# Two of sixteen gates on GpSimd, global q and k loaded to the quarters, and GpSimd's clearing ahead of its loads

## The chip, the core and the metric

The kernel runs on one core of a Trainium2 chip. A core has five engines that run their own instruction streams in order: PE (TensorE, matmuls), DVE (VectorE), ACT (ScalarE), POOL (GpSimd) and SP (SyncE, which issues DMAs). PE writes into PSUM; its weight loads are shown as PEld. GpSimd works on SBUF only and has no operand in PSUM in this kernel. Transfers are issued by SP, ACT or POOL and carried out by sixteen DMA engines. Engines wait for each other by semaphores.

The metric is the device time of one execution in microseconds, as the median of several runs.

## The reference

Eight batches, eight heads, 512 local tokens and 32 global tokens per batch, head dimension 64. Local tokens attend to the global tokens and to a window of 32 tokens on each side; global tokens attend to everything. The joined result goes through a two-layer network with a hard-swish gate.

```
s_g  = scale * q_g @ [k_g, k_l]^T          out_g = softmax(s_g) @ [v_g, v_l]
s_l  = scale * q_l @ [k_g, k_l]^T          local part masked to |i - j| <= 32
out_l = softmax(s_l) @ [v_g, v_l]
x = [out_g, out_l], heads joined           # 8 * 544 rows of 512
h = x @ w_in                               # 512 -> 2048
g = h * clip(h + 3, 0, 6) / 6
out = g @ w_out                            # 2048 -> 512, float32
```

Inputs and output are float32; the kernel works in fp16 with float32 sums in PSUM.

## The kernel before

Attention and network are interleaved. For each batch the attention of the local tokens runs in four pairs of blocks (`local`: scores on PE, `tensor_tensor_reduce` with the mask on DVE for the maximum, exponential on ACT, transposes on PE, values on PE, normalising and a transpose on DVE into `xt`), the global tokens in two halves (`globe`, `globe_values`). Then the first layer of the network (`moe_first`, `first`) makes sixteen chunks of 128 hidden columns: four matmuls into a PSUM bank `m` (three banks), ACT's Relu of (h + 3) / 6 into `t1` (three buffers), and DVE's gate, min(t1, 1) * h, from `t1` and the bank into `gts`. The bank is free when the gate is done. Batch 0 does this in three parts of its tokens, as they come out of attention. The second layer (`moe_second`, `second`) sums sixteen chunks into a bank per 128 tokens, in four quarters of four chunks, copies the bank to `ot` on ACT or DVE, and SP stores it. While PE works on the network of a batch, the attention of the next batch goes on between.

The order of each engine's instructions is fixed when the program is built: a planner (`Plan.lay`) takes operations from named streams, each with a rank and estimated costs, and writes them out one after another. Where an operation may go to several engines, the planner chooses; `SPARE` is a handicap for DVE in this choice. Estimates of a load are its issue, its service and `lat`, the time until it has landed. So ranks and estimates change the order in the program, and nothing else.

Local q and k of batch 0 come in two halves. The first (chunks 0 and 1) is loaded as float32 by SP into a stage in `win`, cast by ACT and turned by DVE into `qt` and `kt`; the second is cast by the transfer itself and is issued by POOL into `wout`. Batch 1's q and k go into `xt` and `qtmp` (turned at line 590 and 595), those of later batches into `rawq` and `rawk`. POOL issues all of these and v, w_in and w_out in one stream, and in the same stream it clears buffer 1 of the keys and values (`clear`, lines 369 to 377), makes the mask's blocks (`band`) and the identity, copies v into the shifted strips `vs` (line 542; ACT and DVE may do so too for batch 0), and from batch 1 on copies key borders (`kg`).

Global q and k of batches 0 and 1 (`once`): one load of 32 rows to partitions 0 to 31, into an `ot` buffer for batch 0 and into `graw` for batch 1, and then four casts of 32 partitions, one for each quarter of `gn`. DVE turns `gn` into `kt` (line 605) and `qg` (line 601). In the program before, ACT issues both loads of batch 0 and SP both of batch 1.

Of the kernel before, what the change touches and what calls it, by code (L numbers as in the profile page):

```python
# [37 lines left out]
class Plan:  # L38
# [7 lines left out]
    SPARE, PHASES = 0.5, 9  # L46
# [146 lines left out]
def kernel(  # L193
# [13 lines left out]
    P = 128  # L207
# [38 lines left out]
    def tiles(name, n, shape, dtype, pool=None):  # L246
        return [(pool or sb).tile(shape, dtype, tag=f"{name}{i}", name=f"{name}{i}") for i in range(n)]
# [10 lines left out]
    graw0 = tiles("graw0_", 1, [W, 2, H, D], FP32)[0]  # L258
# [17 lines left out]
    t1s = tiles("t1", 3, [P, Sl], FP32)  # L276
    ots = tiles("ot", 3, [P, dm], FP32)
# [18 lines left out]
    for name, rank in (("l0", 0), ("ld", 5), ("lq", -2), ("sh", 0), ("sq", 0), ("st", 3.5), ("g0", 0), ("ga", -9), ("first", -9), ("pad", -30), ("gc", -6), ("gd", 3), ("gp", 3.9), ("cast", -5), ("msk", lambda n: 1 if n < 9 else 1.25), ("tq", lambda n: 0 if n < 8 else 3), ("kg", 0.5), ("vs", 1.5), ("clr", 1),  # L296
                       ("s", 0.5), ("mx", lambda n: 1.2 if n < 33 else 2.7), ("ex", 1.9), ("t", -0.5), ("etc", 0), ("av", -0.7), ("nm", 0.7),
                       ("xp", -0.5), ("gx", 1),
                       ("mf", lambda n: 9 + n * 1e-3), ("ms", lambda n: 9 + (n + len(PARTS) * NDFF + 2) * 1e-3), ("t1", 0), ("gate", -0.7), ("ot", 3)):
        plan.stream(name, rank)  # L300
    for name in ("l0", "ld", "lq", "sh", "st", "g0", "ga", "sq"):
        plan.stream("dq" + name, 0 if name in ("l0", "ld", "lq") else -1)
# [56 lines left out]
    def setup():  # L359
        nc.vector.memset(mxs[0], 0.0)  # L360
        clear(nc.vector, 0)
        nc.vector.memset(masks[0], 0.0)
        nc.vector.memset(masks[1][:, 0], 0.0)
        nc.vector.memset(masks[1][:, 1:, W:P - W], 0.0)
        for e in range(2):
            nc.vector.memset(mask(NU)[quarter(e, 0), 0:W], OUTSIDE)
            nc.vector.memset(mask(NU + 1)[quarter(e, 1), P - W:], OUTSIDE)

    def clear(eng, r):
        eng.memset(vg[r], 0.0)  # L370
        eng.memset(vg[r][0:W, :, D:D1], 1.0)
        for e in range(2):
            eng.memset(pairs(kt[r])[quarter(e, 0), :, 0:W, :], 0.0)
# [42 lines left out]

    def stage_loads():
# [3 lines left out]
        there = [[load("g0", "SP", 0.47, 0.65, stage[:, i, c, :], raw(src, 0)[:, c, :], lat=(2.6, 3.1, 3.2, 5.7)[2 * c + i]) for i, src in enumerate((q_l, k_l))]  # L421
# [15 lines left out]
        lower = plan.add("l0", Op(("POOL", 1.9), band))  # L437
        for i, src in enumerate((q_l, k_l)):
            st["qk"][1, i] = [load("l0", "POOL", 0.75, 1.6, nat(0, i)[:, NC // 2:, :], raw(src, 0)[:, NC // 2:, :], lat=4.2 - 0.4 * i)]
        vg_load(0, "l0")  # L440
        for m in (2, 3, NU, 1, 0, NU + 1):
            made["mask", m] = [plan.add("msk", Op(("ACT", 0.21), lambda o=o, i=i: nc.scalar.copy(out=o, in_=i), [lower])) for o, i in places(m)]
# [23 lines left out]
    def once(b, k, src, name):  # L466

        raw_ = (graw0[:, k] if b else ots[k][0:W].rearrange("g (h d) -> g h d", d=D))
        got = load("sh" if b else "ga", "SP" if b else "ACT", 0.47, 0.45 if b else 0.3, raw_, src[b].rearrange("h g d -> g h d"), [w_in_l[1][1]] if b else ())
        g = Buf("gn" + name, 1)  # L470
        state[b]["gn", k] = g
        state[b]["gl"][k] = []
        for e in range(2):
            for f in range(2):
                def cast(engine, e=e, f=f):
                    o, i = gn0[k][quarter(e, f)], raw_.rearrange("g (c e) d -> g e c d", e=2)[:, e]
                    if engine == "ACT":
                        nc.scalar.copy(out=o, in_=i)
                    else:
                        (nc.gpsimd if engine == "POOL" else nc.vector).tensor_copy(out=o, in_=i)  # L480
                op = Op({"POOL": 0.43, "ACT": 0.42} if b else {"ACT": 0.42, "DVE": 0.4} if k else {"ACT": 0.42}, None, [got], [] if e or f else [g])
                op.emit = lambda op=op, cast=cast: cast(op.engine)
                state[b]["gl"][k].append(plan.add("gp" if b else "gc" if k else "gd", op))
# [33 lines left out]
    def v_loads(b, to):  # L517
# [4 lines left out]
        if b == 0:  # L522
            made["ident"] = plan.add("clr", Op(("POOL", 0.55), lambda: make_identity(nc, ident)))
        vl = [load(to, "POOL", 0.88, 1.05 if b else 1.25, lambda j=j: v0[v.slot][:, j, :, 0:D],
                   v_l[b, :, j * P:(j + 1) * P, :].rearrange("h s d -> s h d"), lat=LATE[b] if b else 3.3 - 0.4 * j) for j in range(NJ)]
# [58 lines left out]
    def turn_words(b, st, k):  # L584
# [23 lines left out]
        def halo(c0, c1, e, engine):  # L608
            copy = nc.scalar.copy if engine == "ACT" else nc.gpsimd.tensor_copy
            line = flat(kt[k.slot])  # L610
            for f, at, frm in ((1, 0, 10), (0, 12, 2)):
                copy(out=line[quarter(e, f), c0:c1, at * W:(at + 1) * W],
                     in_=line[quarter(e, 1 - f), c0:c1, frm * W:(frm + 1) * W])
        n = 2 if b == 0 else 1
        for q in range(n):
# [10 lines left out]
            else:  # L626
                st["k"].append(plan.add("tq", Op(("DVE", 1.9 / n), lambda c0=c0, c1=c1: turn_q(c0, c1), st["qk"][q, 0],
                                                 [] if b == 0 else [k])))
                a = plan.add("tq", Op(("DVE", 1.95 / n), lambda c0=c0, c1=c1: turn_k(c0, c1), st["qk"][q, 1]))
                st["k"].append(a)  # L630
            for e in range(2):
                h = Op({"POOL": 0.55, "ACT": 0.5}, None, [a])
                h.emit = lambda h=h, c0=c0, c1=c1, e=e: halo(c0, c1, e, h.engine)
                st["halo"].append(plan.add("kg", h))
# [264 lines left out]
    def first(xfn, n, cs, gfn, deps, takes, reads):  # L899
# [11 lines left out]
        def gate():  # L911
# [5 lines left out]
             for k, c in enumerate(cs)]  # L917
        r = plan.add("t1", Op(("ACT", 0.09 + all_ * 0.00083), lambda: nc.scalar.activation(  # L918
# [33 lines left out]
    def moe_first(b):  # L952
# [4 lines left out]
        for at, part in enumerate(PARTS if b == 0 else [range(NJ)]):  # L957
# [3 lines left out]
            for c in range(0, NDFF, per):  # L961
# [3 lines left out]
                def gated(c=c, g=g, cols=cols, per=per):  # L965
# [3 lines left out]
                            deps, [g] if at == 0 and c % CG == 0 else [], [xt])  # L969
# [24 lines left out]
    with tc.manual_schedule():  # L994
        clean = plan.add("first", Op(("DVE", 0.1), lambda: nc.vector.memset(zero, 0.0)))
        plan.add("pad", Op(("PE", 4.0), lambda: [nc.tensor.matmul(out=aps[0][0:W, 0, 0:2], lhsT=zero, rhs=zero[:, 0:2], start=True, stop=True) for _ in range(100)], [clean],
# [6 lines left out]
        made["clear"] = plan.add("clr", Op(("POOL", 2.4), lambda: clear(nc.gpsimd, 1), [made["ident"]]))  # L1003
# [76 lines left out]
```

## Time and profile before

| | us |
|---|---|
| median of three runs | 327.26 (326.31 to 327.92) |
| the profiled execution | 328.56 |
| its span | 326.8 |
| busy PE / DVE / ACT / POOL | 305.8 / 258.4 / 238.3 / 157.7 |
| xt, batch 1's q: issued / landed | 19.71 / 31.05 |
| gate on DVE (line 914) | 136 of 0.682 |
| Relu on ACT (line 918) | 136 of 0.597 |
| strip copy on POOL, 1056 words | 1.062 |

Times in the profile are microseconds from the span's start. A row of a timeline gives start, length, engine, line, operation, output and input, and how many instructions it joins; in brackets stand the idle time before and what ended it. A row of groups gives the count, the busy time and the mean in ns, and after the second bar the idle time before the group. A DMA row gives the queue, how many transfers, the size, and the time from issue to landing. A stretch's row gives the busy time of PE, PEld, DVE, ACT and POOL (number of instructions in brackets), the granted clock, the share of the sixteen DMA engines, and GB/s. "issue" is time in which an engine waited for nothing that the profile shows.

### The profile page before, as it was taken

Reading aid. Unit: us, or ns where it says so; the run is one execution under the profiler, and the core shown is the slowest. Engines: PE = TensorE matmul, PEld = TensorE weight load, DVE = VectorE, ACT = ScalarE, POOL = GpSimd, SP = SyncE. Lnnn points to the kernel's source line nnn. Section 1 sums busy time; section 2 is a strip of 40 time slices with the busy share of each in tenths; the row PEclk is TensorE's granted clock in tenths of the full one; section 3 lists DMA queues with packets and bytes.
Section 4 is the critical chain, followed back from the end, with each engine's and each line's share of the span. In section 5 each row is a group of like instructions: output and inputs, shape, how many; then the busy total and the mean of one; then the engine's idle time right before and its main releaser. Section 6 shows DMA issues by size and latency. Waiting matters only on the chain.

```text
span 326.8 us, 11215 instructions
## 1 busy us (share of the span) xinstructions
PE 305.8 (94%) x4484; PEld 172.8 (53%) x4484; DVE 258.4 (79%) x913; ACT 238.3 (73%) x550; POOL 157.7 (48%) x205
## 2 busy tenths in 40 slices
PE   4477898799999999999999999999999999999995
PEld 4356784454555545555555555555455545556654
DVE  7788996789989897989998999889989985742210
ACT  7999678557895788868876997699759965643221
POOL 9999999029955935665009944963900000000000
PEclk9999999999999999999999999999999999999999
DMA  8999999959952995199949993999111012011223
GB/s 201 180 215 190 188 212 170 230 152 178 200 85 66 140 184 138 46 111 160 217 118 99 226 138 48 148 157 174 33 35 34 2 34 67 0 34 32 65 53 79
DMA packets 104821, 39.54 MB, mean 121 GB/s; under 512 B 91648, under 2 KB 97536, under 8 KB 104768
## 3 DMA queue, kind: packets, MB, share of 16 engines
q0 software_dynamic: 91392, 16.91, 63.9%
q1 hardware_dynamic: 12832, 21.78, 26.8%
q8 instruction: 35, 0.57, 0.7%
q10 hardware_dynamic: 544, 0.13, 0.2%
q14 instruction: 18, 0.15, 0.2%
HBM read 35.13 MB, written 8.91 MB: 135 GB/s over the span
## 4 chain that ended last, share of the span: by engine, by line
PE 86%; POOL 5%; DMA 3%; DVE 2%; issue 2%; ACT 0%; POOLq 0%
PE m L934 37%; PE m L907 35%; PE t L758 4%; DMA xt<-in_q_l_dram 3%; PE a L776 3%; PE s L699 3%; PE t L847 1%; POOL vs L542 1%; PE s L816 1%; POOL v L308 1%; PE a L857 1%; PE s L712 1%; POOL win L308 1%; DVE qt L590 1%; DVE kt L595 1%
## 5 line engine op out<-in xcount | busy, mean ns | idle before, releaser
L934 PE MATMUL m<-wout,gts 128*128 128x512 f16 (+1 forms) x560 | 130.8, 373 | 1.8 <-issue 1.8
L907 PE MATMUL m<-xt,win 128*128 128x512 f16 (+2 forms) x640 | 121.0, 338 | 2.2 <-DVE gts L914 1.2
L914 DVE SCALAR_TENSOR_TENSOR gts<-t,m 128x512 f16<-128x512 f32 x136 | 92.1, 682 | 34.4 <-ACT t L918 33.1
L918 ACT ACTIVATE t<-m 128x512 f32<-128x512 f32 x136 | 81.2, 597 | 34.5 <-PE m L907 31.4
L907 PEld LDWEIGHTS <-win 128*128 128x128 f16 x704 | 70.4, 114 | 48.0 <-issue 3.8
L542 POOL COPY vs<-v 32x1056 f32<-32x1056 f32 (+4 forms) x91 | 81.7, 898 | 29.1 <-DMA v<-in_v_l_dram 24.8
L749 ACT ACTIVATE ex<-sm,mx 128x128 f16<-128x128 f32 x256 | 84.9, 394 | 7.2 <-DVE mx L743 6.5
L934 PEld LDWEIGHTS <-gts 128*128 128x128 f16 x560 | 51.6, 98 | 52.1 <-issue 3.5
L743 DVE CUSTOM_DVE_ANT_0 sm<-s,mask 128x128 f32<-128x128 f32 x240 | 56.2, 285 | 7.2 <-PE s L712 4.1
L308 POOL DMA_DIRECT2D rawq<-in_q_l_dram x12 | 12.6, 1059 | 46.3 <-DVE rec L785 24.3
L318 ACT COPY et<-t 128x1024 f16<-128x1024 f16 x28 | 28.1, 1005 | 8.1 <-PE t L758 8.0
L308 POOL DMA_DIRECT2D v<-in_v_l_dram x32 | 28.2, 896 | 0.0
L942 ACT COPY ot<-m 128x512 f32<-128x512 f32 (+1 forms) x29 | 16.5, 570 | 15.3 <-PE m L934 15.2
L786 DVE TENSOR_TENSOR x<-a,rec 128x512 f16<-128x512 f32 x32 | 22.1, 692 | 1.1
L799 DVE STREAM_TRANSPOSE xt<-x 128x512 f16<-128x512 f16 x32 | 22.5, 704 | 0.1
L758 PEld LDWEIGHTS <-ex 128*128 128x128 f16 x256 | 17.3, 101 | 9.0 <-ACT ex L749 2.7
L743 DVE DVE_READ_ACCUMULATOR2_ANT mx<- 128x1 f32 x256 | 21.3, 83 | 0.0
L758 PE MATMUL t<-ident,ex 128*128 128x128 f16 x240 | 19.9, 225 | 1.5 <-ACT ex L749 1.5
L318 ACT COPY etg<-t 128x640 f16<-128x640 f16 x16 | 11.1, 692 | 10.5 <-PE t L847 10.5
L776 PEld LDWEIGHTS <-et 128*32 128x32 f16 x1024 | 10.0, 98 | 13.1 <-ACT ex L749 4.7
L646 DVE STREAM_TRANSPOSE qt<-rawq 128x512 f16<-128x512 f16 x24 | 15.5, 680 | 0.0
L650 DVE STREAM_TRANSPOSE kt<-rawk 128x512 f16<-128x512 f16 x24 | 15.5, 679 | 0.0
(92 smaller groups left out, 221.5 us busy)
## 6 DMA issues: line engine op xcount, KB each, us to landing
out_dram<-ot SPq DMA_DIRECT2D x62, 128.0 KB, 2.9
vs<-vg SPq DMA_DIRECT2D x32, 132.0 KB, 5.4
v<-in_v_l_dram POOLq DMA_DIRECT2D x32, 128.0 KB, 6.4
rawq<-in_q_l_dram POOLq DMA_DIRECT2D x12, 256.0 KB, 5.8
rawk<-in_k_l_dram POOLq DMA_DIRECT2D x12, 256.0 KB, 6.8
rawq<-rawq SPq DMA_DIRECT2D x12, 254.0 KB, 5.3
rawk<-rawk SPq DMA_DIRECT2D x12, 254.0 KB, 4.9
win<-in_moe_w_in_dram POOLq DMA_DIRECT2D x4, 512.0 KB, 11.3
```

Source lines behind the costliest of these rows:

```text
L308: eng.dma_start(out=o() if callable(o) else o, in_=i() if callable(i) else i)
L318: nc.scalar.copy(out=o(), in_=i())
L542: (nc.gpsimd if op.engine == "POOL" else nc.vector).tensor_copy(out=o(), in_=i())
L743: nc.vector.tensor_tensor_reduce(out=sms[sm.slot], in0=scored(c // 2)[:, z:z + P], in1=mask(m), scale=-scale, scalar=3.0e38, op0=ALU.add, ...
L749: nc.scalar.activation(out=exs[ex.slot][:, un, c, :], in_=sms[sm.slot], func=EXP, scale=-1.0, bias=mxs[mx.slot])
L758: nc.tensor.matmul(out=turned(tp)[:, z:z + P], lhsT=exs[ex.slot][:, un, c, :], rhs=ident, is_transpose=True)
L786: nc.vector.tensor_tensor(out=xs[x.slot].rearrange("p g (a d) -> p g a d", a=2), in0=o[:, :, 0:D].rearrange("p g (d a) -> p g a d", a=2), ...
L799: nc.vector.transpose(out=xts[xt.slot][:, :, n * P:(n + 1) * P].rearrange("p k (t q) -> p t k q", q=W), in_=xs[x.slot].rearrange("p (t k) ...
L907: nc.tensor.matmul(out=mps[ps.slot][:, k * n:(k + 1) * n], lhsT=column_tile(c)[:, m], rhs=x, start=(m == 0), stop=(m == KC - 1))
L914: nc.vector.scalar_tensor_tensor(out=g, in0=shape(t1s[t1.slot][:, 0:all_]), scalar=1.0, in1=shape(mps[ps.slot][:, 0:all_]), op0=ALU.min, o ...
L918: r = plan.add("t1", Op(("ACT", 0.09 + all_ * 0.00083), lambda: nc.scalar.activation(out=t1s[t1.slot][:, 0:all_], in_=mps[ps.slot][:, 0:al ...
L934: nc.tensor.matmul(out=mps[ps.slot][:, 0:n], lhsT=gfn(c), rhs=w_out_t[c // 4][:, c % 4, cols], start=(c == 0), stop=(c == NDFF - 1))
```

## The change

Several things change together.

- The gate of chunks 5 and 13 of every batch from 1 to 7 (`aside`, 14 gates in all) is made on GpSimd: ACT copies the bank to `t1` as it is, which frees the bank, and GpSimd makes clip(h / 6 + 0.5, 0, 1) * h in three instructions over 128 x 512, with `graw` as work space.
- Global q and k of batches 0 and 1 are loaded to all four quarters of the partitions, by four loads each of 32 rows of 4 heads (every quarter gets the even or the odd heads), and cast by one instruction of 128 partitions. For batch 0 ACT issues two of k's loads, SP two of k's and four of q's; for batch 1 SP issues all eight.
- The identity and the clearing of the second `vg` stand on GpSimd ahead of the second half loads of batch 0's q and k; the rest of the clearing of buffer 1 stands behind them and ahead of the loads of v_g, v and w_in. Before, the clearing stood behind the first w_in load.
- DVE may make mask copies (it takes 7 of 14) and key borders of batch 0. Of the strip copies of batch 0, DVE makes 8 (3 before), ACT 3 (5) and GpSimd 18 (21).
- Turns of batch 1's q stand as four instructions in place of one; three stand ahead of two gates and one behind them.
- Ranks and estimates of the planner change, and with them details of the order on PE, DVE and ACT. The number of matmuls of each kind stays.

```diff
@@ Plan
-    SPARE, PHASES = 0.5, 9
+    SPARE, PHASES = 0.8, 9
@@
-    graw0 = tiles("graw0_", 1, [W, 2, H, D], FP32)[0]
+    graw0 = tiles("graw0_", 1, [P, 2, NC, D], FP32)[0]
+    clip = graw0.rearrange("p k c d -> p (k c d)")
...
-   ("st", 3.5), ("tq", lambda n: 0 if n < 8 else 3), ("vs", 1.5), ("ex", 1.9), ("t", -0.5), ("nm", 0.7), ("xp", -0.5), ("gate", -0.7), ("ot", 3)
+   ("st", 2), ("gq", 0.1), ("tq", lambda n: 1.5 if n < 8 else 4.5), ("vs", 2.2), ("ex", 0.5), ("t", 1), ("nm", 0), ("xp", 1), ("pgate", 0.6), ("gate", -1.4), ("ot", 0)
@@ setup
-        clear(nc.vector, 0)
+        clear_globals(nc.vector, 0)
+        clear_rest(nc.vector, 0)
@@
-    def clear(eng, r):
+    def clear_globals(eng, r):
         eng.memset(vg[r], 0.0)
         eng.memset(vg[r][0:W, :, D:D1], 1.0)
+
+    def clear_rest(eng, r):
@@
+    def mask_part(o, i, lower):
+        op = Op({"ACT": 0.18, "DVE": 0.11}, None, [lower])
+        op.emit = lambda: nc.scalar.copy(out=o, in_=i) if op.engine == "ACT" else nc.vector.tensor_copy(out=o, in_=i)
+        return plan.add("msk", op)
@@ stage_loads
         lower = plan.add("l0", Op(("POOL", 1.9), band))
+        made["ident"] = plan.add("l0", Op(("POOL", 0.55), lambda: make_identity(nc, ident)))
+        plan.add("l0", Op(("POOL", 0.62), lambda: clear_globals(nc.gpsimd, 1)))
         for i, src in enumerate((q_l, k_l)):
-            st["qk"][1, i] = [load("l0", "POOL", 0.75, 1.6, ..., lat=4.2 - 0.4 * i)]
+            st["qk"][1, i] = [load("l0", "POOL", 0.75, 1.6, ..., lat=2.1 - 0.4 * i)]
+        made["clear"] = plan.add("l0", Op(("POOL", 1.9), lambda: clear_rest(nc.gpsimd, 1)))
         vg_load(0, "l0")
@@ once
-        raw_ = (graw0[:, k] if b else ots[k][0:W].rearrange("g (h d) -> g h d", d=D))
-        got = load("sh" if b else "ga", "SP" if b else "ACT", 0.47, ..., raw_, src[b].rearrange("h g d -> g h d"), ...)
-        (four casts, one for each quarter)
+        raw_ = graw0[:, k] if b else ots[k][:, 0:NC * D].rearrange("p (c d) -> p c d", d=D)
+        rows = src[b].rearrange("(c e) g d -> e g c d", e=2)
+        got = []
+        for f in range(2):
+            to, engine = ("sh", "SP") if b else ("ga", "ACT") if k and not f else ("gq", "SP")
+            got += [load(to, engine, 0.47, 0.15, raw_[quarter(e, f)], rows[e], ...) for e in range(2)]
+        def cast(engine):
+            o, i = gn0[k], raw_
...
@@ v_loads
-            made["ident"] = plan.add("clr", Op(("POOL", 0.55), lambda: make_identity(nc, ident)))
@@ turn_words (batch 1)
+                pieces = [(c0, c1)] if b == 0 else [(c, c + 1) for c in range(c0, c1)]
...
@@
+    def gate_aside(x, g):
+        nc.gpsimd.tensor_scalar(out=clip, in0=x, scalar1=1.0 / 6.0, scalar2=0.5, op0=ALU.mult, op1=ALU.add)
+        nc.gpsimd.tensor_scalar(out=clip, in0=clip, scalar1=0.0, scalar2=1.0, op0=ALU.max, op1=ALU.min)
+        nc.gpsimd.tensor_tensor(out=g, in0=clip, in1=x, op=ALU.mult)
@@ first
+        if aside:
+            r = plan.add("t1", Op(("ACT", 0.09 + all_ * 0.00083), lambda: nc.scalar.copy(out=t1s[t1.slot], in_=mps[ps.slot]), a, [t1], [ps]))
+            return plan.add("pgate", Op(("POOL", PG), lambda: gate_aside(t1s[t1.slot], gfn()), [r], takes, [t1]))
@@ moe_first
-                            deps, [g] if at == 0 and c % CG == 0 else [], [xt])
+                            deps, [g] if at == 0 and c % CG == 0 else [], [xt], b > 0 and c % 8 == 5)
@@ the program
-        made["clear"] = plan.add("clr", Op(("POOL", 2.4), lambda: clear(nc.gpsimd, 1), [made["ident"]]))
```

More of the change, by code (lines that the diff above doesn't have):

```diff
@@ L608, in halo @@
         def halo(c0, c1, e, engine):
-            copy = nc.scalar.copy if engine == "ACT" else nc.gpsimd.tensor_copy
+            copy = {"ACT": nc.scalar.copy, "POOL": nc.gpsimd.tensor_copy, "DVE": nc.vector.tensor_copy}[engine]
             line = flat(kt[k.slot])
@@ L995 @@
         clean = plan.add("first", Op(("DVE", 0.1), lambda: nc.vector.memset(zero, 0.0)))
[L996 removed]
+        plan.add("pad", Op(("PE", 1.45), lambda: [nc.tensor.matmul(out=aps[0][0:W, 0, 0:2], lhsT=zero, rhs=zero[:, 0:2], start=True, stop=True) for _ in range(100)], [clean],
                            n=200, mode=("small", "small")))
```

60 lines of the change are left out of this document (28 added, 32 removed).

## The prediction

> **What bounds the kernel now.** I read the stretches first, then the chain that ended last, then the queues of GpSimd and the DMA in the first 35 us. Busy time by stretch (columns: PE, weight loads, DVE, ACT, POOL, clock, DMA share, GB/s):
>
> ```profile
> 35.00:40.00 5.00, 3.54 (x90) 3.41 (x90) 4.97 (x12) 2.37 (x6) 4.37 (x8) 1.00 1.09 192
> ...
> 60.00:100.00 40.00, 40.00 (x601) 20.73 (x600) 35.69 (x121) 29.64 (x66) 23.59 (x26) 1.00 1.13 161
> ...
> 250.00:270.00 20.00, 20.00 (x296) 10.48 (x298) 17.54 (x64) 16.35 (x41) 0.00 (x0) 1.00 0.06 15
> ```
>
> From 60 us on PE is busy without a gap (40.00 of 40, 20.00 of 20). PE's work is the same in both kernels: each kind of matmul comes in the same number. So beyond 60 us nothing can be won, only lost. What can move is the time at which PE becomes full, near 38 us. The chain that ended last says what sets it (start, length, what):
>
> ```profile
> 19.71 11.34 DMA xt<-in_q_l_dram
> 31.08 2.08 DVE qt L590
> 33.15 1.20 DVE gts L914 x2
> 34.51 0.69 DVE x L786
> 35.20 1.98 DVE kt L595 x4
> 37.18 0.53 DVE gts L914
> 37.75 4.69 PE m L907 x56
> ```
>
> The load of batch 1's q into xt lands at 31.05. DVE had finished its work before that at 30.97, turns q (2.08 us), passes the gates that free PE's banks, and at 37.75 PE starts the run that never breaks again but for two waits ("issue", 0.92 us at 51.97 and 1.85 us at 57.24). DVE has no gap between 31 and 43.8, so whatever delays its turn of q delays PE.
>
> The load was issued 11.34 us before it landed: it stood in a queue. GpSimd's order and the DMAs' time from issue to landing:
>
> ```profile
> 2.52 0.84 POOL L308 DMA_DIRECT2D wout<-in_q_l_dram  x1
> ...
> 4.66 3.55 POOL L308 DMA_DIRECT2D v<-in_v_l_dram  x4
> 8.17 0.70 POOL L308 DMA_DIRECT2D win<-in_moe_w_in_dram  x1
> ...
> 10.07 0.30 POOL L373 MEMSET kt<- 32x256 f16 x1
> ...
> 14.80 4.96 POOL L542 COPY vs<-v 32x264 f32<-32x264 f32 x11
> ```
>
> ```profile
> win<-in_moe_w_in_dram POOLq DMA_DIRECT2D x1, 512.0 KB, 9.2
> v<-in_v_l_dram POOLq DMA_DIRECT2D x1, 128.0 KB, 7.0
> ```
>
> The last v load (issued near 7.3) lands at 14.3, the first w_in load (8.17) at 17.4, the fourth at 28.5, xt at 31.05. The DMA engines' share is above 1.0 in every stretch of 1 or 2 us from 3 to 32, so this is one full pipe, and a hole in it is not made good.
>
> **The change part by part.**
>
> Order on GpSimd. Identity and the clearing of vg (8.91 to 10.07, 1.16 us) now stand ahead of the second half loads of batch 0's q and k; the rest of the clearing (10.07 to 12.61, 2.54 us) stands ahead of v_g, v and the first w_in load. So q's half is issued at 2.52 + 1.16 = 3.7 (was 2.52), v_g at 7.8 (4.07), v from 8.4 (4.66), the first w_in at 11.9 (8.17). The second to fourth w_in loads keep 12.6 to 14.8, for the queue up to there holds the same work.
>
> What this does to the pipe: before, v landed 6.5 to 7.0 us after issue, part of it behind other loads. A v load at 53.87, with little ahead of it, took 5.5. So v now lands from 8.4 + 5.5 = 13.9 (was 11.1), and the fourth at 11.0 + 5.5 = 16.5 at best (was 14.3): 2.2 us later. The pipe has run dry meanwhile, since the half loads are through near 9 and v starts arriving past 10. The w_in loads and xt follow in the same queue at its full pace, so they keep their distances: the first w_in 3.1 us behind v (19.6), xt 13.65 us behind that (33.25). The bounds are 31.05 (no hole: the stage loads, alone now, finish early and pull all forward) and 34.3, for if v needs 6.5 us as before, the fourth lands at 17.5. I take the distances from 16.5, since an emptier queue is nearer to the 5.5 row.
>
> Global q and k to the quarters. Each of the four loads of 64 KB becomes four of 32 KB, so the rows come twice: 128 KB more for batch 0, which fit in the hole, and 128 KB more for batch 1, ahead of xt, on a pipe that moved 197 GB/s in the first 62 us: 0.65 us if all of it queued ahead of xt, nothing if it shares engines that are idle. Its packets are small and interleave with w_in's; I take 0.15, near nothing, because the strips and v's packets make the same mix before. SP issues 6 more for batch 0 and 6 more for batch 1 (0.4 to 0.8 us each), in gaps of 7.9 and 19 us between its issues there, so nothing. But batch 0's second k_g copies now queue behind the stage loads on SP: the last stage load lands at 7.6, k_g came at 4.2. The first scores (6.78) move to about 7.6; the second half of k (10.05) and ACT's queue still end that stage, so 0 on the path.
>
> Casts: 16 casts of 0.40 us become 4. ACT had 10 of them and keeps the wide 4, so it saves 6 x 0.40 = 2.4 us before 33 us; POOL saves 4 x 0.41 and DVE 2 x 0.34. DVE takes 7 of the 14 mask copies (about 0.1 each, like its mask memsets of 0.09) and 5 more strip copies (8 instead of 3, about 0.4 each, 2.0 us). None of it is ahead of xt on the path: DVE reaches the turn of q near 31 to 32.5 with or without it. DVE's strip copies now stand in order ahead of the mask-and-maximum instructions and wait for v (13.9 and 14.8, where they ran at 13.4); behind them wait the exponentials, then PE's transposes. That is up to 2.5 us lost in a chain whose ACT part has become 2.4 us shorter: hidden by xt's own lateness, and if that is absent, up to +1.
>
> Turn of q in four pieces: the fourth stands behind two gates, the gate that frees PE at 37.75 still has the same work ahead of it (6.6 us from xt's landing), 0.
>
> Two gates of sixteen, batches 1 to 7 (14 in all). DVE loses 14 x 0.682 = 9.5 us, worth nothing since PE is full. ACT's Relu of 0.597 becomes a copy of about 0.57, nothing. POOL gains 14 gates of three instructions over 128x512. No row of POOL has two inputs. The nearest rows:
>
> ```profile
> L542 POOL COPY vs<-v 32x1056 f32<-32x1056 f32 x42 | 44.6, 1062 | 26.5 <-DMA v<-in_v_l_dram 24.8
> ...
> L542 POOL COPY vs<-v 32x528 f32<-32x528 f32 x7 | 4.4, 623 | 0.3
> ```
>
> Each is between 0.62 and 1.06 us, a gate between 1.9 and 3.2; I take 0.62 + 0.62 + 1.06 = 2.3, as the third reads two tensors and so as many elements as the long copy. The Trainium skill (GPSIMD Engine Reference, 3.1 Elementwise, side by side) measures a two-input add over 2048 elements at 4497 ns, which no row here shows; by it the third would be an estimated 1.1 us and the gate 2.4, with no change in the sum. POOL has 16 of 40 us free (23.59 busy from 60 to 100). Behind a gate on POOL stand strip copies and the raw loads of later batches; the gate itself waits for ACT's copy. PE needs the last such gate (chunk 13) for the fourth quarter of a second-layer tile: two more chunks (1.7 us), three quarters (2.6 us) and two attention pieces (0.8 us), about 5.1 us after its matmuls. ACT 0.6 plus a queued copy 1.06 plus the gate 2.3 is 4.0: fits, 0. If a pair of raw loads (2 x 1.05) or several strips stand ahead, it is late by 0.5 to 1 us in a batch.
>
> DVE sharing memory ports with a busier POOL: the gate on DVE took 682 ns at 62 to 250 us with POOL half busy and 685 ns at 250 to 290 with POOL nearly idle, so 0.
>
> ```profile
> L914 DVE SCALAR_TENSOR_TENSOR gts<-t,m 128x512 f16<-128x512 f32 x86 | 58.3, 682 | 9.2 <-ACT t L918 8.1
> ```
>
> **Sum.** xt lands at 31.05 + 2.2 + 0.15 = 33.4, DVE and PE follow: +2.35 us; the rest 0. The profiled execution took 328.56 (span 326.8), which gives 330.9; it was 1.3 above the median of the runs, 327.26, so on the median I forecast 329.6. A measurement of this kernel tells about 0.5% (1.6 us) from no change.
>
> **The rivals.**
> The hole closes (no change): with q's half issued later the stage loads have the engines alone and every later transfer starts as soon as it is issued; xt is late by the 0.65 of extra rows at most, giving about 327.6. For it: half loads and v shared the engines from 5 to 14. Against: the pipe was full before, so lateness of v adds.
>
> Faster: the two issue waits at 51.97 and 57.24 (2.77 us together) are PE waiting with no engine named, at a time when v's loads at 53.87 fill the DMA queue (share above 2). If everything ahead is shifted against these loads, both waits could go. With 0.65 of extra rows that is 327.26 + 0.65 - 2.77 = 325.1. It decides only when xt is less than about 1.1 us late. Against: the order of those loads and matmuls is almost the same.
>
> Gates late on POOL: 0.5 us in each of seven batches on top of my forecast, 329.6 + 3.5 = 333.1. For it: raw loads cost 1.05 each on POOL and stand ahead of some gates; PE has no slack. Against: 16 of 40 us are free.
>
> **How the numbers follow.** Forecast 0.47, hole closes 0.24, faster 0.14, gates late 0.15. The forecast's own range goes from xt 1.1 us late to 3.9 (34.3 and all 0.65), 328.4 to 331.2; 0.41 of its 0.47 lies over +0.5%, and with the late gates slower is 0.56. The hole closing and the other 0.06 lie within 0.5%: 0.30. Faster is 0.14. The range 325.8 to 333.2 leaves out most of the faster case and the far end of late gates.
>
> **What would show it.** Step by step: v landing from 13.9, the first w_in near 19.6, xt near 33.4; DVE idle about 2 us before its turn of batch 1's q, named for that load; PE's unbroken run starting near 40; PE's total unchanged and full from 62 us; POOL gates near 2.3 us. Wrong would be: xt at 31, PE waiting after 60 us for GpSimd's gates, or the two issue waits gone.

## The result, and the profile after

The changed kernel takes 343.02 us (342.33 to 343.17), the kernel before 327.58 (326.31 to 327.92). The ratio is 1.0475, 95% interval 1.0442 to 1.0508: slower, by 15.4 us where 2.35 were forecast, and outside the range. The profiled execution took 343.17 with a span of 341.4 us, so it stands for the four runs, which lie within 0.9 us.

PE's own work is the same 1264 matmuls of the two layers in both kernels. The moments at which some of them start say in which stage the time goes. Times are from each trace's start; the 192nd matmul of the first layer is the last one of batch 0, and each later column up to the 384th adds 64, a batch. The last column is the time from the 192nd to the last matmul of the second layer.

| kernel | first layer, 1st | 192nd | 256th | 320th | 384th | second layer, last | 192nd to last |
|---|---|---|---|---|---|---|---|
| before | 24.1 | 48.1 | 86.2 | 121.7 | 157.0 | 322.6 | 274.5 |
| after | 27.6 | 51.0 | 91.9 | 131.2 | 170.1 | 336.9 | 285.9 |

So in this execution the start (up to the 192nd) is 2.9 us late, and 11.4 us are lost behind it, where I had forecast nothing. Between the 192nd and the last, PE stands idle for 8.9 us (before: 2.8).

Busy time by stretch, the same three stretches as before (columns: PE, weight loads, DVE, ACT, POOL, clock, DMA share, GB/s):

```profile
35.00:40.00 5.00, 4.06 (x93) 3.39 (x92) 4.97 (x11) 3.68 (x8) 3.17 (x5) 1.00 1.94 184
60.00:100.00 40.00, 37.12 (x469) 18.45 (x469) 28.51 (x103) 26.86 (x60) 24.98 (x26) 0.96 1.24 158
250.00:270.00 20.00, 19.89 (x276) 10.46 (x275) 17.57 (x65) 15.53 (x36) 7.90 (x8) 1.00 0.12 29
```

PE is no longer full from 60 to 100 us: 37.12 of 40, and of these a part runs at a lower clock (0.96 on the mean). The counts, 469 here and 601 before, can't be compared, since another mix of long and short matmuls falls into the 40 us.

The chain that ended last, for the start:

```profile
11.20 6.87 DMA v<-in_v_l_dram
...
20.46 0.47 DVE vs L553
...
33.87 1.57 DVE qt L601 x3
35.45 1.11 DVE gts L936 x2
...
43.44 1.91 PE m L929 x16
45.35 0.67 PE s L726 x62
```

The load of xt isn't in it, but it is no earlier: its landing isn't recorded in this trace, but GpSimd's next load, which waits for it, starts at 34.08, so xt landed near 33.8 (an estimate: 0.28 us lie between the two without the gates, where the landing is recorded). The chain that is shown came at the same moment. v lands at 18.07, DVE's strip copies wait for it, and the attention of batch 0 behind them reaches the turn of batch 1's q at 33.87. PE comes to the scores of batch 1 at 45.35; before, this stood at 42.44, again 2.9 us later.

The groups of the new gate on GpSimd, and the gate on DVE (count, busy us, mean ns, then the idle time before):

```profile
L936 DVE SCALAR_TENSOR_TENSOR gts<-t,m 128x512 f16<-128x512 f32 x122 | 82.6, 683 | 51.2 <-ACT t L943 50.1
L917 POOL TENSOR_SCALAR graw<-t 128x512 f32<-128x512 f32 x14 | 8.6, 613 | 36.5 <-ACT t L941 35.7
L918 POOL TENSOR_SCALAR graw<-graw 128x512 f32<-128x512 f32 x14 | 26.8, 1916 | 1.2
L919 POOL TENSOR_TENSOR gts<-graw,t 128x512 f16<-128x512 f32 x14 | 17.8, 1271 | 1.2
```

A gate is 0.61 + 1.92 + 1.27 = 3.80 us, not 2.3: the instruction with the maximum and minimum takes three times the one with the multiplication and addition. What one such gate does, from the timeline of batch 1 (start, length, engine, line; in brackets the idle time before and what ended it):

```profile
79.38 0.59 ACT L941 COPY t<-m 128x512 f32<-128x512 f32 x1 [0.27 <-PE m L929]
...
79.98 1.06 POOL L553 COPY vs<-v 32x1056 f32<-32x1056 f32 x1
...
81.13 0.61 POOL L917 TENSOR_SCALAR graw<-t 128x512 f32<-128x512 f32 x1
81.83 1.93 POOL L918 TENSOR_SCALAR graw<-graw 128x512 f32<-128x512 f32 x1
83.84 1.26 POOL L919 TENSOR_TENSOR gts<-graw,t 128x512 f16<-128x512 f32 x1
...
85.13 0.60 ACT L943 ACTIVATE t<-m 128x512 f32<-128x512 f32 x1 [2.39 <-POOL gts L919]
...
85.76 0.69 DVE L936 SCALAR_TENSOR_TENSOR gts<-t,m 128x512 f16<-128x512 f32 x1 [2.31 <-ACT t L943]
...
86.50 1.02 PE L929 MATMUL m<-xt,win 128*128 128x512 f16 x4 [1.81 <-DVE gts L936]
...
87.86 4.44 PE L929 MATMUL m<-xt,win 128*128 128x512 f16 x12
```

ACT's copy is ready at 79.97, GpSimd makes a strip first, and the gate ends at 85.10. It holds one of the three t1 buffers as long, so the fourth Relu of ACT behind that copy waits 2.39 us, DVE's gate behind it 2.31, and PE 1.81 for a free bank. After that the twelve matmuls from 87.86 take 4.44 us, 0.37 each, where four just before took 1.02 (0.26). The granted clock had fallen, to 0.50 from 87.86 to 91.27:

```profile
84.00:88.00 4.00, 2.19 (x41) 1.01 (x39) 1.81 (x3) 2.63 (x5) 3.94 (x6) 0.98 1.17 172
88.00:92.00 4.00, 4.00 (x12) 1.45 (x12) 2.54 (x18) 1.80 (x5) 3.72 (x5) 0.59 1.83 197
```

The same happened once more, from 128.82 to 132.23; an estimate from half the clock over these 6.8 us is 3.4 us of PE's time. Over the whole execution ACT waited for GpSimd's gates six times, 9.3 us in all, 2.6 the longest.

### The profile page after: what moved, and what is told of

The parts are those of the page before. It is cut to its first block, busy times and chain, and to the rows that moved or that the text cites. A ratio compares the mean times of both kernels' runs of the same rounds, so it can differ in the third digit from the quotient of the medians.

```text
span 341.4 us, 11276 instructions
## 1 busy us (share of the span) xinstructions
PE 312.1 (91%) x4484; PEld 174.3 (51%) x4484; DVE 249.1 (73%) x906; ACT 234.8 (69%) x539; POOL 210.1 (62%) x242
## 4 chain that ended last, share of the span: by engine, by line
PE 60%; POOL 19%; issue 7%; DVE 6%; DMA 4%; ACT 3%; POOLq 0%; ACTq 0%; DVEq 0%
PE m L959 28%; PE m L929 22%; POOL vs L553 5%; POOL graw L918 5%; POOL gts L919 3%; PE t L772 3%; PE a L790 2%; DMA v<-in_v_l_dram 2%; POOL v L309 2%; DMA wout<-in_k_l_dram 2%; DVE gts L936 2%; POOL graw L917 1%; DVE sm L757 1%; ACT t L943 1%; PE t L861 1%
## 5 line engine op out<-in xcount | busy, mean ns | idle before, releaser
L929 PE MATMUL m<-xt,win 128*128 128x512 f16 (+2 forms) x640 | 126.5, 346 | 5.4 <-DVE gts L936 4.9
L936 DVE SCALAR_TENSOR_TENSOR gts<-t,m 128x512 f16<-128x512 f32 x122 | 82.6, 683 | 51.2 <-ACT t L943 50.1
L943 ACT ACTIVATE t<-m 128x512 f32<-128x512 f32 x122 | 72.5, 599 | 46.7 <-PE m L929 34.5
L929 PEld LDWEIGHTS <-win 128*128 128x128 f16 x704 | 71.3, 115 | 53.6 <-issue 11.0
L553 POOL COPY vs<-v 32x1056 f32<-32x1056 f32 (+5 forms) x88 | 80.4, 913 | 8.9 <-DMA v<-in_v_l_dram 4.2
L319 ACT COPY et<-t 128x1024 f16<-128x1024 f16 x31 | 31.3, 1011 | 7.4 <-PE t L772 7.4
L967 ACT COPY ot<-m 128x512 f32<-128x512 f32 (+1 forms) x34 | 19.5, 574 | 16.7 <-PE m L959 16.2
L917 POOL TENSOR_SCALAR graw<-t 128x512 f32<-128x512 f32 x14 | 8.6, 613 | 36.5 <-ACT t L941 35.7
L918 POOL TENSOR_SCALAR graw<-graw 128x512 f32<-128x512 f32 x14 | 26.8, 1916 | 1.2
L919 POOL TENSOR_TENSOR gts<-graw,t 128x512 f16<-128x512 f32 x14 | 17.8, 1271 | 1.2
```

Source lines behind the costliest of these rows:

```text
L319: nc.scalar.copy(out=o(), in_=i())
L553: (nc.gpsimd if op.engine == "POOL" else nc.vector).tensor_copy(out=o(), in_=i())
L918: nc.gpsimd.tensor_scalar(out=clip, in0=clip, scalar1=0.0, scalar2=1.0, op0=ALU.max, op1=ALU.min)
L919: nc.gpsimd.tensor_tensor(out=g, in0=clip, in1=x, op=ALU.mult)
L929: nc.tensor.matmul(out=mps[ps.slot][:, k * n:(k + 1) * n], lhsT=column_tile(c)[:, m], rhs=x, start=(m == 0), stop=(m == KC - 1))
L936: nc.vector.scalar_tensor_tensor(out=g, in0=shape(t1s[t1.slot][:, 0:all_]), scalar=1.0, in1=shape(mps[ps.slot][:, 0:all_]), op0=ALU.min, o ...
```

## The experiments

Each ratio is to runs of the kernel before on the same chip.

### What is slow in the gate: the two one-input instructions exchanged

```diff
-        nc.gpsimd.tensor_scalar(out=clip, in0=x, scalar1=1.0 / 6.0, scalar2=0.5, op0=ALU.mult, op1=ALU.add)
-        nc.gpsimd.tensor_scalar(out=clip, in0=clip, scalar1=0.0, scalar2=1.0, op0=ALU.max, op1=ALU.min)
+        nc.gpsimd.tensor_scalar(out=clip, in0=x, scalar1=-3.0, scalar2=3.0, op0=ALU.max, op1=ALU.min)
+        nc.gpsimd.tensor_scalar(out=clip, in0=clip, scalar1=1.0 / 6.0, scalar2=0.5, op0=ALU.mult, op1=ALU.add)
```

> The changed kernel with the two one-input instructions of GpSimd's gate exchanged: first clip h to -3..3 (max, min; from t into the work space), then scale and shift in place (mult, add); same result. In the changed kernel the first (mult, add, from t) took 0.613 us, the second (max, min, in place) 1.916. If max and min are what costs, the first now takes 1.92 and the second 0.61; if working in place is what costs, the first takes 0.61 and the second 1.92; both leave the gate at 3.8 and the time near 343. If only the two together cost (max and min in place), both take 0.6, the gate falls to 2.5 and the time to 331 to 335.

343.47 us (343.06 to 343.93), ratio 1.0485 [1.0455, 1.0516]. The maximum and minimum, now first and from `t1`, took 1920 ns, the multiplication and addition, now second and in place, 619. The price goes with the operations, not with the place.

The order is that of the changed kernel, and so this trace also shows what the low clock is worth. PE had the same two gaps (1.84 and 1.98 us), yet the granted clock stayed at 1.00 from 29.6 to 340 us, and the twelve matmuls that took 4.44 us took 2.78:

```profile
87.68 1.02 PE L929 MATMUL m<-xt,win 128*128 128x512 f16 x4 [1.84 <-DVE gts L936]
...
89.03 2.78 PE L929 MATMUL m<-xt,win 128*128 128x512 f16 x12
```

This execution took 343.06 us all the same. Its 192nd matmul starts at 53.6 (5.5 us later than before), and from there to the last it is 283.2 (8.7 more than before). So the low clock isn't needed for the loss, and the split of 2.9 and 11.4 us above belongs to one execution: the start is not equally late in each.

### The gates back to DVE

```diff
-                            deps, [g] if at == 0 and c % CG == 0 else [], [xt], b > 0 and c % 8 == 5)
+                            deps, [g] if at == 0 and c % CG == 0 else [], [xt], False)
```

> The changed kernel with all gates on DVE again, everything else of the change kept. Theory: of the 15.4 us about 2.4 come from the start (v and xt land later) and 13 from the gates; so 327.6 + 2.4 = 330.0, PE without gaps after 62 us, clock 1.00, xt turned near 33.9. Rival: the changed ranks spoil the order of the attention between the chunks; then 334 to 340 with gaps of PE after 60 us that no GpSimd gate explains.

334.87 us (332.71 to 336.20), ratio 1.0216 [1.0167, 1.0265]. So the gates account for 343.0 - 334.9 = 8.1 us, and 7.1 us (ratio 1.0216) are left without any gate on GpSimd. In the profiled execution the 192nd matmul starts at 52.3, 4.2 us later than before, and from there to the last it is 274.1 us (before 274.5): what is left lies in the start. The time is the rival's and not the theory's 330.0, but the rival's gaps of PE after 60 us show only once (1.81 us at 108). This execution, at 332.71, was the fastest of the four, at a granted clock of 1.00; the other three took 2.0 to 3.5 us more, at 0.979 to 0.990, and what they lost there isn't shown. Two of the waits in its first 52 us (engine, line, what it waited for, us in total, times, longest):

```profile
PE s L726 <- DVE kt L616: 5.5, 1, 5.5
ACT gn L491 <- DMA graw<-in_q_g_dram: 3.1, 1, 3.1
```

### Without the gates, and with the clearing behind the first w_in load as before

```diff
-        made["ident"] = plan.add("l0", Op(("POOL", 0.55), lambda: make_identity(nc, ident)))
-        plan.add("l0", Op(("POOL", 0.62), lambda: clear_globals(nc.gpsimd, 1)))
-        made["clear"] = plan.add("l0", Op(("POOL", 1.9), lambda: clear_rest(nc.gpsimd, 1)))
+            made["ident"] = plan.add("clr", Op(("POOL", 0.55), lambda: make_identity(nc, ident)))
+        made["clear"] = plan.add("clr", Op(("POOL", 2.4), clear_all, [made["ident"]]))
```

> As no_gates, and identity and clearing of buffer 1 back behind the first w_in load on GpSimd; the order on PE and ACT stays that of no_gates. Theory (the hole in the DMA queue is the start's loss): v lands from 11 again, xt near 31.2 to 31.7, time 327.6 + 0 to 0.7. Rival (the global loads to the quarters or the new order of the first instructions are the loss): as no_gates, 330.

333.54 us (332.63 to 334.02), ratio 1.0178 [1.0146, 1.0211]. It gives back 1.3 us, the intervals of the two overlap, and the time is above both expectations. The 192nd matmul stays at 52.0. DVE's turn of batch 1's q, first with the clearing ahead (without gates), then with it back:

```profile
31.92 0.70 DVE L813 STREAM_TRANSPOSE xt<-x 128x512 f16<-128x512 f16 x1
33.85 1.59 DVE L601 STREAM_TRANSPOSE qt<-xt 128x256 f32<-128x256 f32 x3 [1.23 <-DMA xt<-in_q_l_dram]
```

```profile
33.51 0.70 DVE L812 STREAM_TRANSPOSE xt<-x 128x512 f16<-128x512 f16 x1
34.13 1.59 DVE L600 STREAM_TRANSPOSE qt<-xt 128x256 f32<-128x256 f32 x3
```

The clearing does move the load: with it xt is issued at 18.99 and lands at 33.83, without it at 19.57 and 30.66. But with xt there in time DVE only comes to the turn at 34.13, out of its own work on batch 0. Two chains are late by the same 3 us, so taking away one of them, my main term, gives back little.

### A buffer of its own for GpSimd's operand

```diff
-        ps, t1 = Buf("m", 1), Buf("t1", 1)
+        ps, t1 = Buf("m", 1), Buf("xc" if aside else "t1", 1)
...
```

> The changed kernel with ACT's copy for GpSimd's gate going to a buffer of its own (one of 128x512) instead of one of the three t1; the gate stays at 3.8 us. Theory (a late gate hurts by holding one of three t1, so that ACT's Relu three chunks later waits, then the banks, then PE): ACT's 9.3 us of waits for the gate and PE's gaps in the first layer go, 333 to 337. Rival (PE waits for the late gates' results themselves in the second layer, or for the strip copies that stand behind them): 341 to 343.

342.55 us (340.75 to 343.06), ratio 1.0441 [1.0394, 1.0488], not clearly less than 1.0475. ACT's waits for the gate are gone from the `t1` ring, but GpSimd is as late, and PE now waits for it directly (PE's waits, 60 to 330 us):

```profile
PE m L960 <- POOL gts L920: 3.8, 3, 2.7
PE a L791 <- POOL vs L554: 2.5, 2, 1.3
PE s L714 <- POOL kt L359: 2.0, 1, 2.0
```

The buffer was only the first place where the lateness of GpSimd came out.

### The gate at the price I had counted

```diff
-        nc.gpsimd.tensor_scalar(out=clip, in0=clip, scalar1=0.0, scalar2=1.0, op0=ALU.max, op1=ALU.min)
+        nc.gpsimd.tensor_scalar(out=clip, in0=clip, scalar1=1.0, scalar2=0.0, op0=ALU.mult, op1=ALU.add)
```

> The changed kernel with the second of the gate's three instructions made a multiplication by 1 and an addition of 0 in place of the maximum and minimum: it leaves the clip out, so the gate is not the hard swish, and every engine's order is the same as in the changed kernel. Theory (what the gates cost is their price: GpSimd's maximum and minimum take 1.92 us where I counted 0.62): a gate of 2.5 to 2.6 us, near the 2.3 that the prediction and the planner used, PE's gaps behind the gates go, and the time comes to what the kernel without gates took, 334 to 336. Rival (any gate on GpSimd comes late, whatever its price, since strip copies and loads stand ahead of it in one queue): 338.5 to 342.

The kernel leaves the clip out of these gates. 334.82 us (333.98 to 337.41), ratio 1.0194 [1.0123, 1.0265], the same as without any gate on GpSimd. The groups of its gate, and two stretches:

```profile
L919 POOL TENSOR_TENSOR gts<-graw,t 128x512 f16<-128x512 f32 x14 | 17.9, 1275 | 1.2
L918 POOL TENSOR_SCALAR graw<-graw 128x512 f32<-128x512 f32 x14 | 8.7, 621 | 1.2
L917 POOL TENSOR_SCALAR graw<-t 128x512 f32<-128x512 f32 x14 | 8.7, 618 | 41.6 <-ACT t L941 40.9
```

```profile
60.00:100.00 40.00, 38.67 (x574) 19.85 (x559) 31.35 (x119) 29.94 (x70) 26.09 (x30) 1.00 1.31 171
100.00:140.00 40.00, 39.15 (x574) 20.05 (x573) 34.50 (x123) 31.43 (x72) 23.83 (x27) 1.00 0.99 117
```

At 2.5 us a gate, in exactly the same order on every engine, the 8 us are gone, and no low clock falls behind 41 us (0.50 stood once, from 37.1 to 40.5, in the start); PE still misses 1.33 and 0.85 us in these two stretches. This shows that the price of one instruction is what the gates cost in this order. It shows as well that gates at 2.5 us win nothing against DVE that these runs can tell. The start is late here too: the 192nd matmul at 52.5.

### The planner told the true price

```diff
-    PG = 2.3
+    PG = 4.0
```

> The changed kernel with the planner told 4.0 us for a gate on GpSimd in place of 2.3, so that it places strips, gates and matmuls by the true price; the work is the same. Theory (the order was written for gates that end 1.6 us earlier than they do): a part of the 8 us comes back, 336 to 340. Rival (GpSimd has too little time between the strips that batch needs, in whatever order): 341 to 344.

338.29 us (337.18 to 338.90), ratio 1.0278 [1.0230, 1.0325]. Against the 343.02 of the changed kernel the order alone gives back 4.7 us (6.5 by the two ratios, whose runs of the kernel before differ by 0.6 us in the median). Over the gates at 2.5 us, measured beside it (334.82), 3.5 us are left. So more than half of the gates' loss came from an order that was written for gates 1.5 us shorter than they are.

### The gates alone, in the kernel before

```diff
...
+        if aside:
+            r = plan.add("t1", Op(("ACT", ...), lambda: nc.scalar.copy(out=t1s[t1.slot], in_=mps[ps.slot]), a, [t1], [ps]))
+            return plan.add("pgate", Op(("POOL", PG), lambda: gate_aside(t1s[t1.slot], gfn()), [r], takes, [t1]))
...
```

> The kernel before with the 14 gates on GpSimd alone (its loads, clearing and ranks stay; the planner writes a new order around the gates, at the same 2.3 us for a gate). Theory (the gate takes 3.9 us, GpSimd's strip copies and its gates come late for PE, whatever stands around them): about 8 us over before, 333 to 338. Rival (they are late only because the new order leaves more for GpSimd late): 327 to 330.

340.21 us (339.84 to 340.46), ratio 1.0391 [1.0364, 1.0418], 12.8 us. More than the theory's 8 and above its range, and PE's gaps are of the same kind (15.68 of 20 us from 80 to 100). Why the gates cost more in the old order than in the new one stays open.

### The loads of the globals alone, in the kernel before

```diff
-        got = load("sh" if b else "ga", "SP" if b else "ACT", 0.47, 0.45 if b else 0.3, raw_, src[b]...)
+            got += [load(to, engine, 0.47, 0.15, raw_[quarter(e, f)], rows[e], ...) for e in range(2)]
...
```

> The kernel before with one part of the change alone: global q and k of batches 0 and 1 loaded to the quarters by four loads each, and one cast for each. Theory (the loads to the quarters make the start late: batch 0's global k lands near 8.4 instead of 4.2 and the first scores wait for it, and ACT stands in its queue for batch 1's global q, which lands near 34): first scores near 9.6, the 192nd first-layer matmul 3 us later than the 48.1 of before, time 330.0 to 331.5. Rival (the new ranks make it late, the loads are hidden): within 1 us of before, 326.8 to 328.3.

331.77 us (330.73 to 332.25), ratio 1.0128 [1.0100, 1.0155]. The chain of its start, and from the view of the tile xt the load and the turn (line 591):

```profile
0.73 3.16 DMA ot<-in_k_g_dram
...
5.87 6.46 DMA ot<-in_q_g_dram
12.43 0.40 ACT gn L479
12.84 0.53 ACT wout L431
```

```profile
L308 POOL DMA_DIRECT2D xt<-in_q_l_dram x1: 769/769/769, 19.9 to 19.9; - x1
L591 DVE STREAM_TRANSPOSE qt<-xt x1: 2064/2064/2064, 34.8 to 34.8; 128x1024 f32<-128x1024 f32 x1
...
DMA to landing us min/median/max: 11.2/11.2/11.2
```

xt lands at 19.9 + 11.2 = 31.1, just as before, and DVE turns it only at 34.8, where it stood at 31.08. What came late is the other chain. Batch 0's global q lands at 12.3, ACT stands waiting for it in its queue, and behind that wait stand a cast of local k and the first exponentials. PE's first scores waited 7.1 us for DVE's turn of global k (before 3.0) and start at 10.8 (before 6.8).

### Of these, batch 0's alone

```diff
+    def once(b, k, src, name):
+        (once_old if b else once_new)(b, k, src, name)
```

> The kernel before with the loads to the quarters and the wide casts for batch 0 alone; batch 1's global q and k stay in the old form. Theory (batch 0's loads cost it: the first scores wait for the second copies of k's rows, and ACT stands waiting for q's, which land near 12.3 behind the stage loads): 330.5 to 332, like both batches' loads together (331.8). Rival (batch 1's loads cost it: they land near 34 and ACT waits for them): 327 to 328.5.

334.67 us (334.08 to 335.21), ratio 1.0171 [1.0125, 1.0217]. So it is batch 0's loads; batch 1's add nothing that shows. That it is over the 1.0128 of both together lies within the two intervals at their ends, and its cause stays open; the time itself is above the theory's 330.5 to 332.

### The changed kernel without gates, with the globals loaded as before

```diff
-            got += [load(to, engine, 0.47, 0.15, raw_[quarter(e, f)], rows[e], ...) for e in range(2)]
...
+        got = load("sh" if b else "ga", "SP" if b else "ACT", 0.47, 0.45 if b else 0.3, raw_, src[b]...)
```

> The changed kernel with all gates on DVE and with global q and k of batches 0 and 1 loaded and cast as before; ranks and the clearing stay changed. Theory (loads to the quarters): it gives back 3 us of the 334.9 that the kernel without gates on GpSimd took, 331 to 332; what is left is the clearing. Rival (order): 334 to 336.

331.67 us (331.16 to 331.92), ratio 1.0127 [1.0104, 1.0150]. It gives back 3.2 us of the 334.87 (2.9 by the two ratios), as the theory said.

### The ranks alone, in the kernel before

```diff
-    SPARE, PHASES = 0.5, 9
+    SPARE, PHASES = 0.8, 9
...
-    ("st", 3.5), ("tq", lambda n: 0 if n < 8 else 3), ("vs", 1.5), ("ex", 1.9), ("t", -0.5), ("nm", 0.7), ("xp", -0.5), ("gate", -0.7), ("ot", 3)
+    ("st", 2), ("tq", lambda n: 1.5 if n < 8 else 4.5), ("vs", 2.2), ("ex", 0.5), ("t", 1), ("nm", 0), ("xp", 1), ("gate", -1.4), ("ot", 0)
```

> The kernel before with the planner's new ranks and its new handicap for DVE, and nothing else. Theory (the loads to the quarters make the start late, not the order): 326.8 to 328.5. Rival (the order makes it late: strips, masks and exponentials stand otherwise on DVE and ACT): 330 to 334.

329.76 us (329.32 to 330.10), ratio 1.0070 [1.0047, 1.0092]: slower than my theory's range, and just short of the rival's. Both held a part: the order costs 2.3 us too. Two pieces of its chain:

```profile
36.06 0.67 DVE top L831
...
37.53 1.97 DVE kt L595 x4
```

The turn of batch 1's q is no later than before (30.66), but a reduction and a transpose now stand ahead of the turn of k, which comes at 37.53 where it stood at 35.20.

### The clearing alone, in the kernel before

```diff
+        made["ident"] = plan.add("l0", Op(("POOL", 0.55), lambda: make_identity(nc, ident)))
+        plan.add("l0", Op(("POOL", 0.62), lambda: clear_globals(nc.gpsimd, 1)))
...
+        made["clear"] = plan.add("l0", Op(("POOL", 1.9), lambda: clear_rest(nc.gpsimd, 1)))
-        made["clear"] = plan.add("clr", Op(("POOL", 2.4), lambda: clear(nc.gpsimd, 1), [made["ident"]]))
```

> The kernel before with one part of the change alone: identity and clearing of the second vg ahead of the half loads of q and k, the rest of the clearing ahead of the loads of v_g, v and the first w_in; nothing else. By the prediction's main step (v's lateness makes a hole in the DMA pipe, xt lands at 33.25): 329.0 to 330.5, with xt landing past 33. Theory now (the loads are late, but xt only by part of it, as xt's distance is set by GpSimd's queue): 327.5 to 329. Both: v landing 2 to 4 us later than the 14.3 of before for its fourth load.

331.09 us against 328.22 of before in that comparison (its runs spread from 326.93 to 331.34), ratio 1.0086 [1.0046, 1.0125]: 2.8 us, between 1.5 and 4.1. The time is above both ranges; on the 327.26 of the earlier comparison the ratio gives 330.1, within the first. The pipe from 9 to 12.5 us, first in the kernel before, then here (the last two columns are DMA share and GB/s):

```profile
9.00:12.50 3.50, 1.10 (x40) 0.93 (x43) 2.63 (x6) 3.33 (x12) 3.14 (x11) 1.00 2.25 161
```

```profile
9.00:12.50 3.50, 0.96 (x32) 0.79 (x35) 2.63 (x6) 3.36 (x11) 3.50 (x5) 1.00 1.12 76
```

The hole is there: 76 GB/s in place of 161. What it does is in the chain:

```profile
11.23 7.43 DMA v<-in_v_l_dram
...
22.27 10.28 DMA xt<-in_q_l_dram
32.57 2.09 DVE qt L594
...
39.17 4.68 PE m L911 x56
```

The fourth v lands at 18.66. GpSimd waits for it 2.39 us with its strip copies, and xt's load stands behind eight of these: it is issued at 22.27, not 19.71, and lands at 32.55, 1.5 us later than before, not past 33. PE's long run starts 1.42 us later (39.17 against 37.75).

### Seven forms of the clip

```diff
-        nc.gpsimd.tensor_scalar(out=clip, in0=clip, scalar1=0.0, scalar2=1.0, op0=ALU.max, op1=ALU.min)
+    FORMS = ((ALU.max, ALU.min), (ALU.max,), (ALU.min,), (ALU.mult,), (ALU.mult, ALU.max), (ALU.max, ALU.add), (ALU.add, ALU.min))
```

> The changed kernel with the second instruction of the 14 gates in seven forms, two gates each: maximum then minimum, maximum alone, minimum alone, multiplication alone, multiplication then maximum, maximum then addition, addition then minimum. It leaves parts of the clip out, so most of its gates are not the hard swish; its time is not used, only the durations of this instruction. Theory (GpSimd computes a maximum or a minimum by another, slower way than a sum or a product, so each costs its own): multiplication alone 0.6 us, one maximum or minimum alone or with a sum or product 1.1 to 1.4 us, both 1.9 us. Rival (any maximum or minimum puts the whole instruction on the slow way): 1.9 us for every form but multiplication alone. Second rival (only the pair is slow): 0.6 us for every form but the pair.

The forms with two operations are the eight on line 923, those with one the six on line 925 (ns, least, median, most):

```profile
L923 POOL TENSOR_SCALAR graw<-graw x8: 1916/1920/1935, 81.9 to 301.7; 128x512 f32<-128x512 f32 x8
```

```profile
L925 POOL TENSOR_SCALAR graw<-graw x6: 1484/1495/1501, 122.9 to 203.1; 128x512 f32<-128x512 f32 x6
```

None of the three expectations holds. Each of the four pairs with a maximum or a minimum takes 1.92 us, also beside a sum or a product; one operation alone takes 1.50, be it maximum, minimum or multiplication; and only multiplication with addition takes 0.62. So a multiplication alone is slower than one with an addition behind it.

## Why the prediction was wrong, step by step

**The price of a gate on GpSimd: the failed step.** I took 0.62 + 0.62 + 1.06 = 2.3 us, with bounds of 1.9 to 3.2, from rows of copies. Measured: 0.61 + 1.92 + 1.27 = 3.80, over the upper bound. With the second at 0.62 in the same order the time was 334.82, so this step cost 8.2 us. The first term was exact, the third 0.2 short, and the second, maximum and minimum, a third of its true value. No row of the trace before had GpSimd do a maximum or minimum, and a copy of like size is no bound for it. By the figure of the Trainium skill (GPSIMD Engine Reference, 3.1 Elementwise, side by side) for 2048 elements the third was an estimated 1.1 us; the measured 1.27 is above it.

**"Fits, 0".** My sum for the last gate was 0.6 + 1.06 + 2.3 = 4.0 against 5.1 us. With 3.8 it is 5.5: the same sum says late. It also left out two things. One is the buffer: the gate holds one of three `t1`, so ACT, DVE and the bank wait long before PE needs the chunk; though giving it a buffer of its own moved the wait and saved little. The other is that a gap of PE can be followed by slow matmuls; but an execution with the same gaps and no low clock was as long.

**The rival "gates late on POOL"** (0.15, 333.1) named the mechanism that took more than half of the loss, with 0.5 us in each of seven batches; measured 8.1 us, 1.2 a batch. What was mis-sized is the lateness, by the step above: at a price of 2.5 us nothing is lost that the runs can show, as my 0 had it. I kept the rows' shares of free time (16 of 40 us) as the argument against it; a queue with 40% free still puts a strip and a gate of 3.8 us one behind the other.

**The start.** Forecast +2.35 by one step, xt landing at 33.4; the kernel without gates on GpSimd is 7.1 us slower. So with the right price of a gate the time (334.8) would still have come out over my range (to 333.2). The step itself came true: xt landed at 33.83 without the gates and 33.60 with gates at 2.5 us, and the fourth v at 15.7 and 16.4 there (forecast 16.5, bound 17.5; 18.07 in the changed kernel's own trace). With the clearing back xt landed at 30.66, so the hole and not the extra rows made it late. Without the gates DVE waited 1.23 us for xt rather than 2, since its own work ended at 32.62 and not at 30.97. In the kernel before, the clearing alone costs 2.8 us (1.5 to 4.1), partly by another way: the fourth v lands at 18.66, GpSimd's strips wait for it, and xt is issued 2.56 us later behind them and lands at 32.55. What the forecast lacked is the other chain to the same turn, which is next.

**"0 on the path" for the globals, and "hidden by xt's own lateness" for the strips: wrong in kind, the second failed step.** I had read that DVE ended its earlier work at 30.97 and that xt landed at 31.05. These are two chains that end within 0.1 us, and I costed only one of them. In the changed kernel both come near 34: xt at 33.8, DVE's own work at 33.87 in one execution and 34.13 with the clearing back. With the globals alone xt is on time and the start is 4.1 us late through the other chain (192nd matmul at 52.2 in place of 48.1), which costs 4.2 us by the ratio. I had even moved k's second copies behind the stage loads and put the first scores at 7.6; with the globals alone they start at 10.8. Global q, behind those copies on the same queue, landed at 12.3, and I had not followed ACT's queue, where the wait for it stops casts and exponentials.

**The ranks** I named only as a change of order and priced at nothing; alone they cost 2.3 us.

These three, alone 2.8, 4.2 and 2.3 us by their ratios, add to 9.3, and together with the untried rest they cost 7.1: they are partly the same delay, as the two turns near 34 show. The mask copies and key borders on DVE and the turn of q in four pieces were not tried alone.

**What held:** xt's lateness; PE full before and so nothing to win (gates at 2.5 us won nothing); DVE's gate unchanged beside a busier GpSimd (683 ns, before 682).

## What to carry to other kernels

Where two chains end at the same moment, price a delay on each; that one is late does not hide the other, and the slack between them is the only cover. Do not price an operation on GpSimd by a copy of the same size: if no row shows that very operation, the upper bound stays open, and the order that a planner writes from a wrong price is a loss of its own. Where one engine is full to the end, work taken off another engine in that stretch wins nothing.

## What was not expected of the hardware

- GpSimd over 128 x 512 float32 words: multiplication with addition 0.62 us, one multiplication, maximum or minimum alone 1.50, each of four pairs with a maximum or minimum 1.92, and the product of two inputs into fp16 1.27.
- TensorE's clock: after 1.81 us without a matmul (84.70 to 86.50) the granted clock was 0.59 from 88 to 92 us, and a matmul of 128 x 512 took 0.37 us on the mean in place of 0.26. The lower clock (0.50) came 1.4 us after PE had started again and lasted from 87.86 to 91.27, 3.41 us. After a gap in 124 to 128 (1.94 us busy of 4) it was 0.71 and then 0.50 in the next two stretches of 2 us; after 1.61 us idle within 164 to 168 it stayed at 1.00. In the trace with the operations exchanged, gaps of 1.84 and 1.98 us at the same places were followed by no lower clock. The Trainium skill (TensorE: Matmul & The Clock Gate, Part 1: The HAM clock gate) describes a window of 3413 ns that runs freely, with the clock halved after an idle one. The 3.41 us at 0.50 agree with its length, and a free run would fit the different outcomes, which no run here shows to be the cause; the gap of 1.81 us shows that less than a whole window without a matmul was enough.
